# Weight statistics as traces on TensorE, later loads of wq and wk, and a new order of the early jobs

## The chip, the cores and the metric

The kernel runs on one core of a Trainium2 chip. The metric is the device time of one execution in microseconds, as the median of several runs. The kernel before takes 695.03 us (three runs, 694.98 to 695.07).

The engines are named as in the profile: PE (TensorE matmul), PEld (its weight loads), DVE (VectorE), ACT (ScalarE), POOL (GpSimd), SP (SyncE, whose queue issues nearly all DMAs).

## The reference

The sum of the input, an attention with a compressive memory, and an MLP, all on one layer norm of the input. 2048 tokens of 512 features, 32 heads of 16, four segments of 512 tokens, a hidden layer of 1792.

```python
x = A_x
xn = _layernorm(x, axis=-1)
return x + _A_ref(xn, A_wq, A_wk, A_wv, A_wo, A_beta) + _B_ref(xn, B_w1, B_b1, B_w2, B_b2)

# _A_ref, per segment s and head:
logits = einsum(qs, ks) * scale + mask            # keys at or before the query
a_dot = softmax(logits) @ vs
a_mem = (phi(qs) @ M) / (phi(qs) . z + 1e-6)      # memory of the earlier segments
o = g * a_mem + (1 - g) * a_dot;  M += phi(ks)^T vs;  z += sum(phi(ks))
...
return concat(o) @ wo
# _B_ref: y = layernorm(xn); return gelu(y @ w1 + b1) @ w2 + b2
```

## The kernel before

Everything in float32 is split into two float16 numbers, a high part and the rest, and each product is made of three matmuls (high by high, high by low, low by high). For that each weight matrix, in parts, goes through three steps before it can be used:

- `wl` (`w_load`, line 247): SP loads the raw float32 weights. They lie in the same memory that will hold the split weights, two pieces further on, or in a stage borrowed from another tile.
- `wm` (`w_square`, line 287): a sum of squares of the part, one number for each of 128 partitions. ACT squares the values (line 311) with an accumulator, which a second instruction reads.
- `wf` (`w_scale` and `qk_scale`): one or more matmuls with a matrix of ones add the partitions, ACT takes the root by logarithm and exponential (lines 320 and 321), and a few small DVE operations round it to a power of two and derive the scales.
- `ws` (`w_split`, line 358): the split of one piece of 128 x 512. In mode V, ACT writes the scaled high part (line 366) and DVE subtracts it from the scaled raw piece (line 367). In mode G, POOL scales (line 369), ACT copies to float16 (line 370), POOL subtracts (line 371).

The parts are `qk` (the first of four column pieces of wk and wq, for the first unit), `QK` (the other three), `v`, `1a` and `1b` (the halves of w1), `2a` and `2b` (the halves of w2) and `o`. `LOADS`, `SQUARES` and `SPLIT` (lines 43 to 46) say how many steps each has, and in what mode its pieces are split.

The work on data is cut into 16 units for the attention (segment by group of eight heads) and 16 for the MLP (256 tokens by half of the hidden layer). The jobs are: `X` and `Xt` layer norm and transposes, `T` the projection of a unit's queries or keys (12 matmuls of 512 columns, with copies on ACT and DVE and DMAs by SP that write strips to memory and read them back), `N` transposed keys, `V` values, `M` the maximum over logits (matmuls and a DVE reduction, line 628), `R` rows of maxima, `S` logits and their exponential, `pv` weights by values, `O` normalization, `D` seven hidden-layer matmul groups of a unit (12 matmuls of 256 columns and a DVE operation, line 756), `G` and `H` the activation and its split, `e` the second MLP layer, `out` the output projection, `A` the loading of the residual. `warm` is a job of eight matmuls on a matrix of ones (line 828) whose result is not used; there are 14 of them.

The order of all jobs is written out by hand, not found at run time: `streams()` makes one list for each kind, `ORDER` is a string with one letter for each job, and the letter says from which list the next job comes (a is the first list, c is `wts`, the loads; i is `maxi`, t is `warm`; the lists of the weight parts come last). Every engine and the SP queue execute their own instructions in this order, each waiting for what it needs. `BANKS` gives the PSUM bank of each accumulator in the same way.

In `ORDER` of the kernel before, 12 of the 14 warm-up jobs stand before the first projection T(0,1), all squares of qk and QK are spread among them, and the loads go: x, qk, QK, v, small ones, 1a, 2a, 1b.

Of the kernel before, what the change touches and what calls it, by code (L numbers as in the profile page):

```python
# [19 lines left out]
P = 128  # L20
# [8 lines left out]
NG = H // GH  # L29
# [9 lines left out]

PARTS = ("qk", "QK", "v", "1a", "2a", "1b", "2b", "o")
LOADS = {"qk": 1, "QK": 3, "v": 2, "1a": 2, "2a": 2, "1b": 3, "2b": 2, "o": 2}
SQUARES = {"qk": 2, "QK": 6, "v": 2, "1a": 3, "2a": 2, "1b": 4, "2b": 4, "o": 3}
SPLIT = {"qk": "VV", "QK": "GVGVGV", "v": "VVVV", "1a": "GVGVGVG", "2a": "GVGVGVG", "1b": "GVGVGVG", "2b": "GVGVGVG",
         "o": "GVGV"}
OFF = [0, 512, 1024, 896]
LEN = [512, 384, 256, 128]
SWAP = [(i + 16) % 32 for i in range(32)]
# [7 lines left out]
def streams():  # L57
    keys, queries, nat, maxi, soft, vals_p, heads, memo, vals, norm, again, hid, act, mlp, outs, accs, wts = (
        [] for _ in range(17))
    for i in range(NU):  # L60
        s, g = divmod(i, NG)
        keys.append(("T", i, 1))
        queries.append(("T", i, 0))
        maxi += [("M", i, n) for n in range(12)] + [("R", i)]
        for h, ts in enumerate(((0, 2), (1, 3))):
            soft += [("S", i, t, n) for t in ts for n in range(3)]
            vals_p += [("pv", i, h, kb) for kb in range(3)] + [("PV", i, h)]
        heads += [("O", i, k) for k in range(3)]
# [12 lines left out]
    again = [("ratio", n) for n in range(NSEG)]  # L81
    for j in range(NU):
        hf, fh = divmod(j, 2)
        hid += [("D", j, f) for f in range(FH)]
        act += [("G", j)] + [("H", j, c) for c in range(4)]
        if fh == 0:
            accs += [("A", 2 * hf + a, k) for a in range(2) for k in range(2)]
        mlp += [("e", j, n) for n in range(2 * FH)]
    for m in PARTS:
        wts += [("wl", m, k) for k in range(LOADS[m])]  # L90
        if m == "qk":
            wts.append(("hold",))
# [9 lines left out]
ORDER = (
    "aatcucuccvavtctveecttcetcuvaactvuvtaatcattavdtubcwwvccfwxxcxwxyxyxxgyhxcoxxvwxofooowcvwzyzoiyyiazgyyziiynzoiiys"
    "ppAnziiniicvzvcniiooAzmAihiiopzqqiqcivpqjpqjijqqijizqjiqqjiiAwszBzoAskkkkmjiAojoijsoAijAqjqjasAfoAopgkkkkpjpjqq"
    "jlpoolojjjooilihAAkkkkpaiqqiqijqjqqijqjiqjqjisBfgpiiqkkkkmpliqqiooiqpBlqoBopohijjiojiijpolsjiqaqajqiqiqqiiqapka"
    "kmkktspaqijqiqjqiqajqbqajopijjgBfopkkkBkjjjlooooBlhjjjolqiqqiipkkkkjiqqijqqjjiqiqjjqiqiqiBkkkkmpliilfnplimpngrr"
    "mrjjponijqjqjinjipiskmkkmkaiijrijjoojiqsjqqjiqiiiqqkkkkihlqlfmlogojqjqjqqjjasoojmkkkkmqjiqjqjjaojjpipmooisikkkk"
    "lpilhiofmgoooqiqpppqiqiqqqiiiqqpsosmoiqqiiqiqppsslooijqjojijojijoiaakkkkmpaijqjqjaqqqjiqqjiqjqiikmkkakbqiaqqahl"
    "olfqjjojqmjgjjoolmmkkkkmhjjoojjiitjiojiippkkkkliiilnfnimpligniinipmrrijjrsijqjqiqjiqjqiipkmkkksiqjqijqjqjiqjqii"
    "qjqikmpkkkiprlqsphlfojmjgopjjlojpjoomokmkkkqiqisjojiqisjqiqijqqijqhiqqiiqjsqiiqppmkkkkilalofomqpgopaoooospmlajq"  # L110
    "qqjqqjqjqiiqiqqqjqiqqipipooooiijooppoiaakkkkmajiqpisqqjiqjqjaiqaqhjqqqjqaaqmkkkkbjlfoljqjmjgojjqolmkkkkmmjjjooj"
    "jioijoiiippkpkkkiinliifniiilnnimlgrpmjjrmjjjrrijikkpskkiqqijqiqijqqjiqjiqjqiqjiqiispqkpkskksqilqoplfojmjgjjjpoo"
    "oojolmkkkkiqjiqpsjiqiqijqjqiqijqjiqiqiqiiqqkksmkpikplolfjjqmjgjjjoooooklpkmkkjiiopjqiqijqjiqpjqiqijqiqqiqiiqikk"
    "pspkkqiplpoooopljjjqqqjqjjqooolkpskmkpkmqqqpqjpjqqqjqjqpqqjqjqqqkmkkkqlllqqqqqqqqqrrrr"
)

BANKS = (
    "012345670123457063571265407321640573216405732164053271640527163054271630542713605427105472105427105472105472015"  # L120
    "470251407251405712470512470512470536124075631254076340125637123756123576132576132576132576132576135402761350427"
    "163054273106542736574326574326537425632754632574631072456310724563071245360712453620731620731067203617621073621"
    "073621073621037621037621037261702361475023671540263701524603175246031746013746013713460713471630471630463714067"
    "314056723410523674105236741052367410527410527410527410527410527140352671450326475103264751023674523674523647253"
    "647236547236475264735264107532410765324107265431067512043675120436751204736152047361520473615270346150312750317"
    "250317253107250371257013275027135027134650132754062751340621375460376054370567403056374065374065307645307645307"
    "642153076241076241076241076253410762534621075346210754316024310264310432610432610324610324612403246013752640163"
    "754207156437120564371205647312056473120564731206547321065473265104723607423460273460273642073642073642051736420"
    "157642031765420316750316705315631705630157630157630157306173504621357462017345620147536210436024136024316403216"
    "403216403216403216740536740536740536740536271406"  # L130
)


# [14 lines left out]
def infini_mixer_kernel(ctx: ExitStack, tc: tile.TileContext, x, wq, wk, wv, wo, beta, w1, b1, w2, b2, out):  # L148
    nc = tc.nc
    V, A, G, T, Q = nc.vector, nc.scalar, nc.gpsimd, nc.tensor, nc.sync  # L150
# [13 lines left out]
    def dense():  # L164
        return dps.tile([P, 512], F32, name="ps" + next(bank), bufs=1)
# [73 lines left out]
    def columns(w, c, n=1):
# [3 lines left out]
        return t.rearrange("p (k c) -> p k c", k=KT)  # L243

    def w_load(m, k):
        if m in ("qk", "QK"):
            g = 0 if m == "qk" else 1 + k
            for w in "kq":
                if g == 2:
                    t = sb.tile([P, 1280], F32, name="pt", bufs=4)  # L250
                    stage[w] = t[:, :512], t[:, 512:1024]
                Q.dma_start(four(piece(w, g)), columns(SRC[w], g))  # L252
            return
# [31 lines left out]
        V.memset(piece("k", 1)[:, :1], 0.0)  # L285

    def w_square(m, k):
        if m in ("qk", "QK"):
            w, g = part(m, k)
            r, junk, to = piece(w, g), WT[w][:, 1], am[:, NG * "kq".index(w) + g:NG * "kq".index(w) + g + 1]  # L290
        else:
# [19 lines left out]
        A.activation(junk.bitcast(BF)[:, :r.shape[1]], r, AF.Square, accum_out=to)  # L311

    def floor2(dst, src):

# [44 lines left out]
    def w_split(m, n):  # L359
        w, c = part(m, n)  # L360
        s = qkcol(1, "kq".index(w), c) if w in "kq" else \
            col({"v": SV, "o": SO, "1": S1, "2": S2}[w] + (m[1:] == "b"))
        r = piece(w, c)
        h, l = WT[w][:, c, 0, :], WT[w][:, c, 1, :]
        if SPLIT[m][n] == "V":
            A.activation(h, r, AF.Copy, scale=s)
            V.scalar_tensor_tensor(l, r, s, h, op0=OP.mult, op1=OP.subtract)
        else:
            G.tensor_scalar(r, r, s, 0.0, op0=OP.mult, op1=OP.add)
            A.activation(h, r, AF.Copy)  # L370
            G.tensor_tensor(l, r, h, op=OP.subtract)  # L371
# [539 lines left out]
```

## Time and profile before

| what | value |
|---|---|
| median of three runs | 695.03 us (694.98 to 695.07) |
| span of the profiled execution | 693.1 us |
| instructions in it | 16949 |
| PE busy | 678.7 us, 98% |
| DVE busy | 535.4 us, 77% |
| ACT busy | 522.7 us, 75% |
| POOL busy | 347.2 us, 50% |
| DMA | 55.12 MB, mean 80 GB/s |

The profile is of one execution. Its span, from the first to the last instruction that the profiler saw, is 693.1 us; no other time of that execution is given. The runs' median lies 1.9 us above it. A busy PE is not PE at its peak: matmuls are pipelined, their recorded durations overlap, and a group's cost is best read from the start of one group to the start of the next. In rows of a timeline the columns are start, length, engine, line, operation, what is written and read, shapes and count; in brackets stands the idle time of the engine before it and who ended it.

### The profile page before, as it was taken

What the parts mean: (1) busy time and instruction counts of PE and PEld (TensorE: products, weight loads), DVE (VectorE), ACT (ScalarE), POOL (GpSimd) and SP (SyncE); (2) the same over time, 40 slices, a digit from 0 to 9 for tenths busy, and PEclk for the clock granted to TensorE, in tenths of its full rate; (3) what the DMA queues carried; (4) which work ended last, traced back from release to release, by engine and by line L of the source; (5) the groups of instructions that cost most, each with busy time, mean ns of one, the idle gap of its engine ahead of it and who ended that gap; (6) DMA issues with size and microseconds to landing.
All of it is one profiled execution on the core that took longest, in us unless ns stands there. A gap on an engine that the chain in (4) does not pass through costs nothing.

```text
span 693.1 us, 16949 instructions
## 1 busy us (share of the span) xinstructions
PE 678.7 (98%) x6359; PEld 395.7 (57%) x6359; DVE 535.4 (77%) x1695; ACT 522.7 (75%) x1013; POOL 347.2 (50%) x533
## 2 busy tenths in 40 slices
PE   7799999999999999999999999999999999999997
PEld 6465556576654555566554456567564456656653
DVE  4499978897795887998798786888678595969442
ACT  5989898878795659857795697757795687778870
POOL 5276768365624425664334445454362546455752
PEclk9899999999999999999999999999999999999999
DMA  9984222420204213431113224231120416140101
GB/s 272 283 238 136 64 63 63 108 62 14 84 10 115 87 44 74 100 71 33 51 45 92 63 72 99 63 93 33 31 80 24 132 18 152 18 108 3 18 1 61
DMA packets 51790, 55.12 MB, mean 80 GB/s; under 512 B 4782, under 2 KB 40636, under 8 KB 51708
## 3 DMA queue, kind: packets, MB, share of 16 engines
q1 hardware_dynamic: 49404, 49.84, 25.3%
q0 software_dynamic: 2304, 4.20, 3.7%
q8 instruction: 50, 0.82, 0.5%
q14 instruction: 32, 0.26, 0.1%
HBM read 36.99 MB, written 17.04 MB: 78 GB/s over the span
## 4 chain that ended last, share of the span: by engine, by line
PE 78%; ACT 10%; POOL 4%; DVE 3%; issue 2%; DMA 1%; SPq 1%; POOLq 0%; ACTq 0%; DVEq 0%
PE ps L480 33%; PE ps L797 16%; PE ps L690 10%; PE ps L815 6%; PE ps L661 5%; PE ps L621 5%; ACT pt L666 2%; DVE ps L628 2%; PE ps L571 2%; PE ps L499 1%; ACT hT L763 1%; ACT hT L771 1%; SPq L252 1%; POOL w1s L371 1%; DMA pt<-in_A_wk_dram 1%
## 5 line engine op out<-in xcount | busy, mean ns | idle before, releaser
L628 DVE CUSTOM_DVE_ANT_0 ps<-ps,mask 128x512 f32<-128x512 f32 (+3 forms) x512 | 233.8, 522 | 16.1 <-PE ps L621 14.9
L666 ACT ACTIVATE pt<-ps,qkcs 128x512 f32<-128x512 f32 (+1 forms) x384 | 206.1, 624 | 35.3 <-PE ps L661 33.5
L797 PE MATMUL ps<-w2s,hT 64*128 64x512 f16 x1344 | 176.7, 376 | 0.2
L480 PE MATMUL ps<-xnT,w1s 128*128 128x256 f16 x1344 | 157.8, 273 | 0.0
L675 POOL TENSOR_SCALAR_AFFINE_SELECT pt<-pt 128x256 f32<-128x256 f32 x256 | 99.1, 414 | 92.0 <-ACT pt L666 91.0
L480 PEld LDWEIGHTS <-w1s 128*128 128x128 f16 x1344 | 127.3, 98 | 29.1 <-issue 11.3
L772 POOL TENSOR_TENSOR hT<-hh,hT 128x512 f16<-128x512 f32 x64 | 67.8, 1059 | 82.8 <-ACT hT L771 81.0
L797 PEld LDWEIGHTS <-hT 64*128 64x128 f16 x1344 | 76.3, 94 | 50.7 <-issue 6.0
L690 PE MATMUL ps<-pt,vt 128*32 128x512 f32 (+3 forms) x1024 | 77.3, 435 | 0.1
L756 DVE SCALAR_TENSOR_TENSOR hT<-ps,sc,sr 128x256 f32<-128x256 f32 x112 | 52.1, 478 | 27.2 <-PE ps L480 27.0
L628 DVE DVE_READ_ACCUMULATOR2_ANT mc<- 128x1 f32 x512 | 70.6, 138 | 0.0
L661 PE MATMUL ps<-qst,kst 50*128 50x512 f16 (+3 forms) x512 | 67.5, 298 | 0.3 <-ACT pt L666 0.2
L621 PE MATMUL ps<-kst,qst 48*128 48x256 f16 (+3 forms) x512 | 67.1, 297 | 0.5
L771 ACT ACTIVATE hT<-hh 128x512 f16<-128x512 f32 x64 | 36.6, 572 | 33.4 <-POOL hh L770 32.9
L690 PEld LDWEIGHTS ps<-pt,vt 128*32 128x32 f32 x1024 | 31.3, 109 | 42.4 <-issue 30.8
L770 POOL TENSOR_SCALAR hh<-hT,sc 128x512 f32<-128x512 f32 x64 | 41.8, 653 | 26.6 <-ACT hT L763 24.9
L720 POOL TENSOR_TENSOR nN<-nN,oT 128x512 f32<-128x512 f32 x16 | 20.3, 1267 | 61.3 <-DVE oT L546 61.3
L763 ACT ACTIVATE hT<-hT,b1t 128x256 f32<-128x256 f32 x112 | 46.4, 495 | 0.2
L480 PE MATMUL ps<-xnT,wqs 128*128 128x512 f16 x192 | 45.6, 389 | 0.0
L480 PE MATMUL ps<-xnT,wks 128*128 128x512 f16 x192 | 44.3, 379 | 0.0
L480 PE MATMUL ps<-wvs,xnT 128*128 128x512 f16 x192 | 44.0, 380 | 0.1
L815 PE MATMUL ps<-wos,oT 128*128 128x512 f16 x192 | 43.2, 380 | 0.6 <-POOL oT L726 0.6
(217 smaller groups left out, 890.0 us busy)
## 6 DMA issues: line engine op xcount, KB each, us to landing
kd<-hl SPq DMA_DIRECT2D x48, 128.0 KB
qd<-hl SPq DMA_DIRECT2D x48, 128.0 KB
kst<-kd SPq DMA_DIRECT2D x32, 192.0 KB
qst<-qd SPq DMA_DIRECT2D x32, 192.0 KB
acc<-in_A_x_dram SPq DMA_DIRECT2D x16, 256.0 KB
acc<-in_B_b_dram POOLq DMA_DIRECT2D x16, 256.0 KB, 4.1
out_dram<-acc SPq DMA_DIRECT2D x16, 256.0 KB
xt<-in_A_x_dram SPq DMA_DIRECT2D x14, 256.0 KB
```

Of the source, the lines that this page charges most:

```text
L480: T.matmul(p, wsl(ws, k, a), xsl(xs, k, b), start=s0 and i == 0, stop=s1 and i == 3 * n - 1)
L621: T.matmul(p[:, o:o + n], stk[i, 0][r, t, P * qb:P * qb + P], stk[i, 1][r, t, :n], start=True, stop=True)
L628: V.tensor_tensor_reduce(p[:, o:o + n], p[:, o:o + n], mask[:, 512 - n:], 1.0, -3e38, OP.add, OP.max, mc[:, 16 * b + 4 * t + qb:16 * b + 4 ...
L661: T.matmul(p[:, o:o + n], stk[i, 1][r, t, P * kb:P * kb + P], stk[i, 0][r, t, P * kb:], start=True, stop=True)
L666: A.activation(e[:, OFF[kbs[0]]:OFF[kbs[0]] + o], p[:, :o], AF.Exp, scale=qkcs[:, 1, i % NG:i % NG + 1])
L675: G.affine_select(v, v, pattern=[[0, 2], [1, P]], compare_op=OP.is_ge, fill=0.0, base=0, channel_multiplier=-1)
L690: T.matmul(p[32 * c:32 * c + 32, P * kb:], vt[s, kb][:, 4 * g + c, 16 * odd:16 * odd + 32], pt[i, 2 * c + odd][:, OFF[kb]:OFF[kb] + LEN[kb ...
L756: V.scalar_tensor_tensor(hz[:, fi, :], p[:, :256], col(F1 + fh), srow[hs][:, own], op0=OP.mult, op1=OP.mult)
L763: A.activation(z, z, AF.Gelu_apprx_tanh, bias=b1t[:, FH * (j % 2) + f:FH * (j % 2) + f + 1])
L772: G.tensor_tensor(hT[:, z, 1, :], t, hT[:, z, 0, :], op=OP.subtract)
L797: w = T.matmul(pes[j][a], hTs[fh][r, fi, u, P * a:P * a + P], w2s[r, fo, v, :], start=n == 0 and m == 0, stop=fi == FH - 1 and m == 2, ski ...
L815: T.matmul(p, o[:, u, P * b:P * b + P], wos[:, g, v, :], start=i == 0, stop=i == 3 * NG - 1)
```

## The change

The sums of squares of qk, QK, v, 1a and 2a (all but that of the bias b1) are no longer made on ACT. Each block of 128 columns of the raw weights, read as the upper halves of its float32 values (bfloat16), is multiplied with its own transpose on PE, and the products are added up in one PSUM bank; the sum of squares is the trace of that matrix, which DVE takes with a multiplication by the identity and a sum along the row.

QK is now the second column piece alone; the third and the fourth are a new part, RK, with loads of its own that stand later in the order, a scale of its own and a list of its own. The job that computes the gates moves from the list of v to that of RK.

A new mode P of the split has POOL write the scaled high part as float16 at once, and DVE subtract. It takes the place of G, and of some V, in QK, RK, v, 1a and 2a: counting the two V of qk, which stay, 15 pieces are P and 11 are V, where 11 were G and 15 V.

The first 270 jobs come in a new order; from T(3,1) on the order is that of before. Four of the twelve warm-up jobs that precede T(3,1) now stand after T(0,1): two right behind it, one behind D(0,6), one behind T(2,1). The loads go: x, qk, QK, v, small ones, 1a, 2a, then RK in two steps (behind T(0,1) and behind T(0,0)), 1b. The seven jobs D(0,0) to D(0,6) come before the first M. The letters of the weight lists shift by one, since u is now the list of RK's loads.

```diff
@@ -39,11 +39,12 @@
 
 
 
-PARTS = ("qk", "QK", "v", "1a", "2a", "1b", "2b", "o")
-LOADS = {"qk": 1, "QK": 3, "v": 2, "1a": 2, "2a": 2, "1b": 3, "2b": 2, "o": 2}
-SQUARES = {"qk": 2, "QK": 6, "v": 2, "1a": 3, "2a": 2, "1b": 4, "2b": 4, "o": 3}
-SPLIT = {"qk": "VV", "QK": "GVGVGV", "v": "VVVV", "1a": "GVGVGVG", "2a": "GVGVGVG", "1b": "GVGVGVG", "2b": "GVGVGVG",
+PARTS = ("qk", "QK", "v", "1a", "2a", "RK", "1b", "2b", "o")
+LOADS = {"qk": 1, "QK": 1, "RK": 2, "v": 2, "1a": 2, "2a": 2, "1b": 3, "2b": 2, "o": 2}
+SQUARES = {"qk": 2, "QK": 2, "RK": 4, "v": 2, "1a": 3, "2a": 2, "1b": 4, "2b": 4, "o": 3}
+SPLIT = {"qk": "VV", "QK": "PV", "RK": "PPPP", "v": "VPVP", "1a": "PVPVPVP", "2a": "PVPVPVP", "1b": "GVGVGVG", "2b": "GVGVGVG",
          "o": "GVGV"}
+TRACES = ("qk", "QK", "RK", "v", "1a", "2a")
 OFF = [0, 512, 1024, 896]
 LEN = [512, 384, 256, 128]
 SWAP = [(i + 16) % 32 for i in range(32)]
@@ -87,47 +88,48 @@
             accs += [("A", 2 * hf + a, k) for a in range(2) for k in range(2)]
         mlp += [("e", j, n) for n in range(2 * FH)]
     for m in PARTS:
-        wts += [("wl", m, k) for k in range(LOADS[m])]
+        if m != "RK":
+            wts += [("wl", m, k) for k in range(LOADS[m])]
         if m == "qk":
             wts.append(("hold",))
         if m == "v":
             wts.append(("par",))
     split = [[("wm", m, k) for k in range(SQUARES[m])] + [("wf", m)] + [("ws", m, c) for c in range(len(SPLIT[m]))] +
-             [("gate",)] * (m == "v") for m in PARTS]
+             [("gate",)] * (m == "RK") for m in PARTS]
     zero = [("zero", 0), ("const",), ("zero", 1)]
     return [norm, again, wts, [("par2",)], zero, keys, queries, nat, maxi, soft, vals_p, heads, memo, vals, hid, act,
-            mlp, outs, accs, [("warm", n) for n in range(14)]] + split
+            mlp, outs, accs, [("warm", n) for n in range(14)], [("wl", "RK", k) for k in range(2)]] + split
 
 
 ORDER = (
-    "aatcucuccvavtctveecttcetcuvaactvuvtaatcattavdtubcwwvccfwxxcxwxyxyxxgyhxcoxxvwxofooowcvwzyzoiyyiazgyyziiynzoiiys"
...
+    "atacctcaetcttetcawvavcatwvcaxeacatxvdccwvxwfttyyyxbxyyuxgyyyzozoywouoxyccyzhoAzzAootAAppciiizAznpBiiABfBncAiBpi"
+    "gzBszniipnzBiimchqqqiCBqBqiiioAoACBCCBCjjqiojqAjqjcioijoiCikskkBcmDskioBjiqiqCjjoijqCiqjsCqjDiftaoCCpgkkkpkjqCj"
+    "oloojjljoloojiipkkkkiqihspqijqqipqijqiqjsjqqjaajfgpiiqkkkkmpliqqiooiqpDlqoDopohijjiojiijpolsjiqaqajqiqiqqiiqapk"
+    "akmkktspaqijqiqjqiqajqbqajopijjgDfopkkkDkjjjlooooDlhjjjolqiqqiipkkkkjiqqijqqjjiqiqjjqiqiqiDkkkkmpliilfnplimpngr"
+    "rmrjjponijqjqjinjipiskmkkmkaiijrijjoojiqsjqqjiqiiiqqkkkkihlqlfmlogojqjqjqqjjasoojmkkkkmqjiqjqjjaojjpipmooisikkk"
...
 )
 
 
 
 BANKS = (
-    "012345670123457063571265407321640573216405732164053271640527163054271630542713605427105472105427105472105472015"
...
+    "050123614061756123401632157467410534702651305176254301741260523716405142730612547306651240651024615024612504612"
...
 )
 
 
@@ -228,12 +230,12 @@
         n = PIECES[m]
         return flat(m)[:, 512 * c + 1024:512 * c + 1536] if c < n - 2 else stage[m][c - n + 2]
 
+    QKG = {"qk": 0, "QK": 1, "RK": 2}
+
     def part(m, c):
 
-        if m == "qk":
-            return "kq"[c], 0
-        if m == "QK":
-            return "kq"[c % 2], 1 + c // 2
+        if m in QKG:
+            return "kq"[c % 2], QKG[m] + c // 2
         return m[0], c + (FH if m[1:] == "b" else 0)
 
     def columns(w, c, n=1):
@@ -243,8 +245,8 @@
         return t.rearrange("p (k c) -> p k c", k=KT)
 
     def w_load(m, k):
-        if m in ("qk", "QK"):
-            g = 0 if m == "qk" else 1 + k
+        if m in QKG:
+            g = QKG[m] + k
             for w in "kq":
                 if g == 2:
                     t = sb.tile([P, 1280], F32, name="pt", bufs=4)
@@ -285,7 +287,7 @@
         V.memset(piece("k", 1)[:, :1], 0.0)
 
     def w_square(m, k):
-        if m in ("qk", "QK"):
+        if m in QKG:
             w, g = part(m, k)
             r, junk, to = piece(w, g), WT[w][:, 1], am[:, NG * "kq".index(w) + g:NG * "kq".index(w) + g + 1]
         else:
@@ -308,7 +310,17 @@
             junk = junk.rearrange("p n a c -> p (n a c)")
         else:
             junk = junk.rearrange("p a c -> p (a c)")
-        A.activation(junk.bitcast(BF)[:, :r.shape[1]], r, AF.Square, accum_out=to)
+        if m not in TRACES or r is b1t:
+            A.activation(junk.bitcast(BF)[:, :r.shape[1]], r, AF.Square, accum_out=to)
+            return
+        p = dense()
+        v = r.bitcast(BF).rearrange("p (c a) -> p c a", a=2)[:, :, 1]
+        n = r.shape[1]
+        for c in range(0, n, P):
+            u = v[:, c:min(c + P, n)]
+            T.matmul(p[:u.shape[1], :u.shape[1]], u, u, start=c == 0, stop=c + P >= n)
+        c = min(P, n)
+        V.tensor_tensor_reduce(p[:c, :c], p[:c, :c], ident[:c, :c], 1.0, 0.0, OP.mult, OP.add, to[:c])
 
     def floor2(dst, src):
 
@@ -333,8 +345,8 @@
         V.scalar_tensor_tensor(qkcs[:, 1, g0:g0 + n], f[:, 0], float(2 ** 10), f[:, 1], op0=OP.mult, op1=OP.mult)
 
     def w_scale(m):
-        if m in ("qk", "QK"):
-            return qk_scale(*((0, 1) if m == "qk" else (1, NG - 1)))
+        if m in QKG:
+            return qk_scale(QKG[m], 1 + (m == "RK"))
         h = m[1:] == "b"
         nb = m[0] == "1"
         n = 4 if h else 3 if m == "o" else 2
@@ -362,7 +374,10 @@
             col({"v": SV, "o": SO, "1": S1, "2": S2}[w] + (m[1:] == "b"))
         r = piece(w, c)
         h, l = WT[w][:, c, 0, :], WT[w][:, c, 1, :]
-        if SPLIT[m][n] == "V":
+        if SPLIT[m][n] == "P":
+            G.tensor_scalar(h, r, s, 0.0, op0=OP.mult, op1=OP.add)
+            V.scalar_tensor_tensor(l, r, s, h, op0=OP.mult, op1=OP.subtract)
+        elif SPLIT[m][n] == "V":
             A.activation(h, r, AF.Copy, scale=s)
             V.scalar_tensor_tensor(l, r, s, h, op0=OP.mult, op1=OP.subtract)
         else:
```

More of the change, by code (lines that the diff above doesn't have):

```diff
@@ L102 @@
 ORDER = (
-    "aatcucuccvavtctveecttcetcuvaactvuvtaatcattavdtubcwwvccfwxxcxwxyxyxxgyhxcoxxvwxofooowcvwzyzoiyyiazgyyziiynzoiiys"
[L104 to L112, printed above, removed]
@@ L113 @@
-    "oojolmkkkkiqjiqpsjiqiqijqjqiqijqjiqiqiqiiqqkksmkpikplolfjjqmjgjjjoooooklpkmkkjiiopjqiqijqjiqpjqiqijqiqqiqiiqikk"
-    "pspkkqiplpoooopljjjqqqjqjjqooolkpskmkpkmqqqpqjpjqqqjqjqpqqjqjqqqkmkkkqlllqqqqqqqqqrrrr"
+    "atacctcaetcttetcawvavcatwvcaxeacatxvdccwvxwfttyyyxbxyyuxgyyyzozoywouoxyccyzhoAzzAootAAppciiizAznpBiiABfBncAiBpi"
+    "gzBszniipnzBiimchqqqiCBqBqiiioAoACBCCBCjjqiojqAjqjcioijoiCikskkBcmDskioBjiqiqCjjoijqCiqjsCqjDiftaoCCpgkkkpkjqCj"
+    "oloojjljoloojiipkkkkiqihspqijqqipqijqiqjsjqqjaajfgpiiqkkkkmpliqqiooiqpDlqoDopohijjiojiijpolsjiqaqajqiqiqqiiqapk"
@@ new lines @@
+    "akmkktspaqijqiqjqiqajqbqajopijjgDfopkkkDkjjjlooooDlhjjjolqiqqiipkkkkjiqqijqqjjiqiqjjqiqiqiDkkkkmpliilfnplimpngr"
+    "rmrjjponijqjqjinjipiskmkkmkaiijrijjoojiqsjqqjiqiiiqqkkkkihlqlfmlogojqjqjqqjjasoojmkkkkmqjiqjqjjaojjpipmooisikkk"
+    "klpilhiofmgoooqiqpppqiqiqqqiiiqqpsosmoiqqiiqiqppsslooijqjojijojijoiaakkkkmpaijqjqjaqqqjiqqjiqjqiikmkkakbqiaqqah"
+    "lolfqjjojqmjgjjoolmmkkkkmhjjoojjiitjiojiippkkkkliiilnfnimpligniinipmrrijjrsijqjqiqjiqjqiipkmkkksiqjqijqjqjiqjqi"
+    "iqjqikmpkkkiprlqsphlfojmjgopjjlojpjoomokmkkkqiqisjojiqisjqiqijqqijqhiqqiiqjsqiiqppmkkkkilalofomqpgopaoooospmlaj"
@@ L115 @@
+    "qqqjqqjqjqiiqiqqqjqiqqipipooooiijooppoiaakkkkmajiqpisqqjiqjqjaiqaqhjqqqjqaaqmkkkkbjlfoljqjmjgojjqolmkkkkmmjjjoo"
+    "jjioijoiiippkpkkkiinliifniiilnnimlgrpmjjrmjjjrrijikkpskkiqqijqiqijqqjiqjiqjqiqjiqiispqkpkskksqilqoplfojmjgjjjpo"
+    "ooojolmkkkkiqjiqpsjiqiqijqjqiqijqjiqiqiqiiqqkksmkpikplolfjjqmjgjjjoooooklpkmkkjiiopjqiqijqjiqpjqiqijqiqqiqiiqik"
+    "kpspkkqiplpoooopljjjqqqjqjjqooolkpskmkpkmqqqpqjpjqqqjqjqpqqjqjqqqkmkkkqlllqqqqqqqqqrrrr"
 )
 BANKS = (
-    "012345670123457063571265407321640573216405732164053271640527163054271630542713605427105472105427105472105472015"
@@ L121 @@
[L121 to L130, printed above, removed]
+    "050123614061756123401632157467410534702651305176254301741260523716405142730612547306651240651024615024612504612"
@@ new lines @@
+    "504650124650412650412650412650142650142650421607653420107642531076425031702531270531270531270132570132570132576"
+    "135402761350427163054273106542736574326574326537425632754632574631072456310724563071245360712453620731620731067"
+    "203617621073621073621073621037621037621037261702361475023671540263701524603175246031746013746013713460713471630"
+    "471630463714067314056723410523674105236741052367410527410527410527410527410527140352671450326475103264751023674"
+    "523674523647253647236547236475264735264107532410765324107265431067512043675120436751204736152047361520473615270"
@@ new lines @@
+    "346150312750317250317253107250371257013275027135027134650132754062751340621375460376054370567403056374065374065"
+    "307645307645307642153076241076241076241076253410762534621075346210754316024310264310432610432610324610324612403"
+    "246013752640163754207156437120564371205647312056473120564731206547321065473265104723607423460273460273642073642"
+    "073642051736420157642031765420316750316705315631705630157630157630157306173504621357462017345620147536210436024"
+    "136024316403216403216403216403216740536740536740536740536271406"
```

## The prediction

> **What bounds the kernel now.** I read the page first, then the busy time by stretch, then the timeline of each engine in the first 124 us.
>
> ```profile
> span 693.1 us, 16949 instructions
> ...
> PE 678.7 (98%) x6359; PEld 395.7 (57%) x6359; DVE 535.4 (77%) x1695; ACT 522.7 (75%) x1013; POOL 347.2 (50%) x533
> ...
> PE   7799999999999999999999999999999999999997
> ...
> ACT  5989898878795659857795697757795687778870
> ...
> PEclk9899999999999999999999999999999999999999
> ```
>
> PE is the bound from the third slice on. The first two slices are different: much of what PE does there is warm-up (line 828), and one slice shows a lower clock. The stretches below are cut at three marks: A, 19.18 us, where the first key projection starts on PE; B, 33.96, the first hidden-layer job D(0,0); C, 123.52, the key projection T(3,1). From T(3,1) on the job order of the two kernels is the same, 1038 jobs, so what the change is worth is by how much C moves.
>
> ```profile
> 0.00:19.18 19.18, 15.18 (x121) 12.67 (x122) 8.88 (x30) 11.95 (x31) 8.93 (x23) 1.00 0.96 274
> 19.18:33.96 14.78, 9.88 (x49) 5.55 (x46) 6.00 (x28) 14.47 (x27) 4.35 (x5) 0.77 0.96 295
> 33.96:80.00 46.04, 45.54 (x382) 26.40 (x380) 44.64 (x151) 41.75 (x83) 31.50 (x37) 1.00 0.55 159
> 80.00:123.52 43.52, 43.52 (x457) 26.86 (x457) 34.05 (x106) 39.38 (x80) 30.59 (x48) 1.00 0.23 57
> 123.52:693.10 569.58, 564.62 (x5361) 324.26 (x5358) 441.86 (x1383) 415.13 (x797) 271.80 (x422) 1.00 0.24 63
> ```
>
> Columns: length, then busy time of PE, PEld, DVE, ACT, POOL, granted clock, DMA share, GB/s. From A to B ACT is busy 14.47 of 14.78 us: it squares and splits weights, and PE waits for it. From B to 80 us PE (45.54 of 46.04) and DVE (44.64) are both full; from 80 to C PE alone.
>
> ```profile
> 17.86 1.05 PE L828 MATMUL ps<-ones 128*128 128x256 f16 x8
> 18.75 0.60 PE L433 MATMUL ps<-ident,rat 128*128 128x128 f32 x4
> 19.18 2.91 PE L480 MATMUL ps<-xnT,wks 128*128 128x512 f16 x12
> 21.93 0.71 PE L343 MATMUL ps<-am,ones 128*128 128x1 f32 x4
> 25.95 0.59 PE L343 MATMUL ps<-am,ones 128*128 128x1 f32 x2 [3.31 <-ACT w1s L311]
> 27.77 0.59 PE L343 MATMUL ps<-am,ones 128*128 128x1 f32 x2 [1.23 <-ACT w1s L311]
> ...
> 28.64 4.18 PE L480 MATMUL ps<-xnT,wqs 128*128 128x512 f16 x12
> ...
> 33.25 0.38 PE L343 MATMUL ps<-am,ones 128*128 128x1 f32 x2 [0.31 <-ACT w2s L311]
> 33.56 0.47 PE L499 MATMUL ps<-ident,phk 64*128 64x64 f32 x8
> 33.96 2.79 PE L480 MATMUL ps<-xnT,w1s 128*128 128x256 f16 x24
> 36.59 2.75 PE L480 MATMUL ps<-xnT,wks 128*128 128x512 f16 x12
> 39.18 5.40 PE L480 MATMUL ps<-xnT,w1s 128*128 128x256 f16 x48
> ```
>
> ```profile
> 50.78 1.14 PE L343 MATMUL ps<-am,ones 128*128 128x1 f32 x8
> 51.78 0.36 PE L345 MATMUL ps<-am,ones 128*128 128x1 f32 x2
> ...
> 123.52 2.76 PE L480 MATMUL ps<-xnT,wks 128*128 128x512 f16 x12
> ```
>
> PE's real work from A to B: two projections at 2.75 (row 36.59; the one at 28.64 took 4.18 at a clock of 0.77), 14 matmuls of scales (21.93 to 33.25) at 0.125 (eight from 50.78 to 51.78), and 0.40 of transposes (33.56 to 33.96): 5.5 + 1.75 + 0.4 = 7.65. So 14.78 - 7.65 = 7.1 us are lost to ACT. That, and what lies ahead of A, is all that the change can win before B.
>
> **The change part by part.**
>
> *ACT.* 14 squares with their accumulator reads leave ACT (8 of 512 columns, two of 1024, four of 1792), and 15 of its 26 copies for splits. At the rows of two of them (1.70 us for 1792 columns, 0.63 for 512, below) that is about 5 + 2 + 7 for squares and 9 for copies. ACT no longer limits anything up to B. Worth nothing by itself where PE is full, so it counts as the 7.1 us above.
>
> ```profile
> 9.81 0.63 ACT L311 ACTIVATE wks<-wks 128x512 bf16<-128x512 f32 x1 [0.27 <-DMA wks<-in_A_wk_dram]
> ...
> 10.44 0.19 ACT L397 ACTIVATE nw<-nw 128x8 f32<-128x8 f32 x1
> ...
> 16.41 2.01 ACT L469 ACTIVATE xnT<-ps 128x512 f16<-128x512 f32 x4
> ...
> 24.10 1.70 ACT L311 ACTIVATE w1s<-w1s 128x1792 bf16<-128x1792 f32 x1
> ```
>
> ```profile
> 8.07 0.53 DVE L396 TENSOR_SCALAR nw<-ag 128x4 f32<-128x4 f32 x1
> ...
> 33.84 0.75 DVE L367 SCALAR_TENSOR_TENSOR w1s<-w1s,sc 128x512 f16<-128x512 f32 x1 [3.68 <-ACT w1s L366]
> ...
> 37.92 0.81 DVE L367 SCALAR_TENSOR_TENSOR w1s<-w1s,sc 128x512 f16<-128x512 f32 x1 [0.39 <-ACT w1s L366]
> 38.65 1.17 DVE L367 SCALAR_TENSOR_TENSOR wqs<-wqs,qksc 128x512 f16<-128x512 f32 x1
> ...
> 49.17 0.32 DVE L628 CUSTOM_DVE_ANT_0 ps<-ps,mask 128x128 f32<-128x128 f32 x1
> 49.42 0.13 DVE L628 DVE_READ_ACCUMULATOR2_ANT mc<- 128x1 f32 x1
> ```
>
> *Mark A.* The norm's logarithm waited on ACT from 8.60 (8.07 + 0.53) to 10.44 behind squares, and the four copies into xnT from the transposes' end to 16.41. Now neither waits. What stands in front is PE's own queue: the first trace needs the second key piece, whose landing ACT saw at 9.81; from there, in order, 12 + 4 + 16 traces (below: 0.08 each, 2.6), four groups of transposes at 0.43 (row 18.75 to 19.18: 1.7), two warm-up jobs at 0.89 (17.86 to 18.75: 1.8) and the first scale 0.25: 9.81 + 6.35 = 16.2. Then DVE has the last trace's reduction (0.25) and the key split (0.75): 17.2 with no gap. Upper end: 19.18, as before. I take 18.0, since DVE has the first scale's chain and four xnT halves to pass in the same time: -1.2.
>
> *Traces on PE.* A piece of n columns takes n/128 matmuls of 128x128, each with its own weights. After A stand 28 of w1, 28 of w2, 16 of the later wq and wk: 72. No such matmul is in the trace. Bounds: half of a 256-column one with its own weights (row 39.18: 5.40/48 = 0.1125, half 0.056), and the f32 transposes of 128 columns (0.43/4 = 0.108). The middle, 0.08, is what I take, since the columns say the first and a weight load per matmul the second: 72 x 0.08 = +5.8 (4.0 to 7.8).
>
> *Warm-up jobs.* Before, all 12 that precede C stand before A, where PE has nothing else. Now eight do; two follow T(0,1), one follows D(0,6), one T(2,1). 4 x 0.89 = +3.6 if PE has work to do there, nothing if it would wait.
>
> *Small ones on PE.* The row-scale transposes move behind A (+0.43), the scale of wv ahead of it (four at 0.125, -0.5), RK has a scale of its own (two, +0.25): +0.2.
>
> *DVE.* 11 more subtractions (0.75: 8.3), 14 reductions of traces at 0.25 (49.17 to 49.42: 3.5), six small operations for RK at no more than that (1.5): +13.3 on 93.6 (8.88 + 6.00 + 44.64 + 34.05), that is 106.9 by C. From A, with some 10 done before it, 97 of the 106.8 us that the sum below leaves: 91%. It fits, but the stretch B to 80 stays as full as it was; so I let the waits that it hides stay as they are.
>
> *POOL.* 22 operations of the old G splits (0.69 and 1.2) become 15 P's.
>
> ```profile
> 32.73 0.69 POOL L369 TENSOR_SCALAR w1s<-w1s,sc 128x512 f32<-128x512 f32 x1
> 34.41 1.20 POOL L371 TENSOR_TENSOR w1s<-w1s 128x512 f16<-128x512 f32 x1 [0.98 <-ACT w1s L370]
> ...
> 38.15 1.13 POOL L369 TENSOR_SCALAR w1s<-w1s,sc 128x512 f32<-128x512 f32 x1
> ```
>
> POOL gets freer by 22 x 0.95 - 15 x 0.69 = 10 us. But each P runs beside DVE's subtractions. The trace has that pairing: POOL's 38.15 took 1.13 instead of 0.69, DVE's 38.65 1.17 instead of 0.75, while DVE's 37.92, also beside it, took 0.81. DVE is free enough up to B (6.00 of 14.78 busy), so the eight P's of 2a and RK count: between 8 x 0.06 = 0.5 and 8 x 0.42 = 3.4. I take 0.5, the price of the pair in which DVE was first; the 9% of DVE's time that are free can take up the rest.
>
> [...]
>
> *Queues.* SP: the loads of RK (four of 256 KB) leave their place before wv. At about 295 GB/s (row A to B) 1.05 MB come 3.6 us earlier for wv, w1, w2. Nobody waited for them (the square at 24.10 shows no idle time before it), so that hides. RK's loads now stand behind the strip DMAs of T(0,1) and T(0,0), which wait for ACT and DVE; behind them are the loads of 1b, and RK's traces wait for them after D(0,4). The strips of T(0,0) leave SP some 7 us after it in the old trace, and PE has D(0,0) to D(0,4) for as long: hidden, and if not, a delay of 1 to 2 us. POOL's queue gets nothing new to issue.
>
> **The sum.** C after = 18.0 + 7.65 + 89.56 (B to C as it was) + 5.8 + 3.6 + 0.2 = 124.8, against 123.52: +1.3. With 0.5 for POOL beside DVE: +1.8. The span of the profiled execution is 693.1; the runs' median is 695.03, 1.9 above it, so I add the difference to the median: 696.8. In words: the 7.1 us that PE lost to ACT, and 1.2 at the start, are filled with 9.6 us of new matmuls that stand in PE's own queue.
>
> **The rivals.**
>
> 1. *The fillers are free* (faster). If PE would wait at those four places for DVE or for a landing, the warm-up jobs cost nothing. For: the two after T(0,1) stand before traces whose sum DVE must first reduce behind T(0,1)'s own evictions. Against: w1 has landed by then, and PE is never idle from B to C. 696.8 - 3.6 = 693.2; it decides when 3.2 of the 3.6 are free.
> 2. *Traces at the low end* (no change). At 0.056 they cost 4.0: 696.8 - 1.8 = 695.0. For: weight loads lie beside matmuls everywhere (PEld 57% beside PE 98%). Against: here each matmul is as short as its load.
> 3. *DVE becomes the bound* (slower still). With the full 0.42 on eight P's 1.3 + 3.4 gives 699.7. For: DVE is at 97% from B to 80 already. Against: ACT, which it waited for, is free. [...]
>
> **How the numbers follow.** What a measurement of this kernel can tell from no change is about 0.2%, 1.4 us. Forecast 0.42, of which 0.30 lies above +1.4 us and 0.12 below it; rival 1 0.22; rival 2 0.22; rival 3 0.14. Faster 0.22, same 0.12 + 0.22 = 0.34, slower 0.30 + 0.14 = 0.44. The likeliest case by itself: 695.6 to 698. The range goes down to rival 1 with part of rival 2's saving, 692.7, and up to rival 3 with the traces in the middle, 699.8.
>
> **What would show it.** A at 17 to 19; about 72 new 128x128 matmuls after it at 0.06 to 0.11, without ACT as releaser of the scale matmuls; D(0,0) at about 30 instead of 33.96 (18.0 + 2.75 + 1.8 + 28 traces 2.2 + 0.43 + 0.75 + 2.75 + 14 traces 1.1 = 29.8), yet T(3,1) at 124 to 126. Line 367 on DVE longer than 0.75 in the mean, and P's longer than 0.69. I am wrong if PE shows idle time of 2 us or more between A and 50 us in which the warm-ups hide, if T(3,1) comes before 122, or if the stretch after T(3,1) does not take 569.6.

## The result, and the profile after

The changed kernel takes 691.43 us (median of four runs, 691.08 to 691.68), the kernel before, beside it, 695.0 (694.78 to 695.07). The ratio is 0.9945, 95% interval 0.9931 to 0.996: faster by about 3.6 us. The forecast was 696.8, on the other side of no change, and the time lies below the range that was given. Two more sets of runs of the same kernel, on other chips, gave 692.28 (ratio 0.9965, 0.9953 to 0.9978) and 692.11 (0.9959, 0.9947 to 0.9971); they are the measure for the experiments that ran beside them.

The page of the changed kernel, the lines that answer to those shown of before:

```profile
span 689.8 us, 17163 instructions
...
PE 681.8 (99%) x6465; PEld 399.8 (58%) x6465; DVE 545.7 (79%) x1740; ACT 502.9 (73%) x972; POOL 340.5 (49%) x526
...
PE   8999999999999999999999999999999999999997
...
ACT  4486897788786659856794796766795687878870
...
PEclk9999999999999999999999999999999999999999
```

PE's second slice is now full, ACT's first two went from 5 and 9 to 4 and 4, and no slice has a lower clock. The stretches between the marks A (T(0,1) starts on PE), B (D(0,0)), 80 us and C (T(3,1)); columns as before: length, then PE, PEld, DVE, ACT, POOL, granted clock, DMA share, GB/s.

```profile
0.00:15.95 15.95, 13.80 (x122) 11.70 (x123) 9.77 (x42) 6.83 (x13) 8.95 (x23) 1.00 0.95 275
15.95:26.36 10.41, 10.41 (x95) 7.39 (x95) 9.47 (x35) 5.43 (x15) 3.06 (x4) 1.00 1.01 326
26.36:80.00 53.64, 52.89 (x505) 33.77 (x506) 51.46 (x177) 38.41 (x79) 27.88 (x37) 1.00 0.55 161
80.00:120.20 40.20, 40.20 (x408) 23.54 (x395) 31.94 (x102) 35.83 (x70) 26.96 (x41) 1.00 0.31 74
120.20:689.80 569.60, 564.53 (x5360) 323.40 (x5358) 443.10 (x1387) 416.39 (x799) 273.68 (x424) 1.00 0.24 63
```

A moved from 19.18 to 15.95, B from 33.96 to 26.36, C from 123.52 to 120.20, and the stretch after C takes 569.60 against 569.58. So C's 3.32 us are the whole change in the span (693.1 to 689.8). All of it was there at A already (3.23): from A to C the kernel before took 104.34, the one after 104.25. Within that, A to B is 4.4 shorter (14.78 to 10.41) and B to C 4.3 longer (89.56 to 93.84). In the profiles of the two other sets C is at 120.70 and 120.18. PE in that first part:

```profile
9.44 0.62 PE L321 MATMUL ps<-wks 128*128 128x128 bf16 x8 [0.55 <-DMA wks<-in_A_wk_dram]
...
10.57 1.04 PE L843 MATMUL ps<-ones 128*128 128x256 f16 x8
...
13.68 1.04 PE L843 MATMUL ps<-ones 128*128 128x256 f16 x8
...
15.10 0.23 PE L855 MATMUL ps<-ident,mhl 14*128 14x14 f32 x1
15.26 0.38 PE L338 MATMUL ps<-am,ones 128*128 128x2 f32 x2
15.50 0.58 PE L355 MATMUL ps<-am,ones 128*128 128x1 f32 x4
15.95 2.75 PE L495 MATMUL ps<-xnT,wks 128*128 128x512 f16 x12
18.53 1.91 PE L843 MATMUL ps<-ones 128*128 128x256 f16 x16
20.28 1.77 PE L321 MATMUL ps<-w1s 128*128 128x128 bf16 x28
21.89 0.60 PE L448 MATMUL ps<-ident,rat 128*128 128x128 f32 x4
22.32 0.56 PE L355 MATMUL ps<-am,ones 128*128 128x1 f32 x4
...
22.96 2.75 PE L495 MATMUL ps<-xnT,wqs 128*128 128x512 f16 x12
25.55 0.97 PE L321 MATMUL ps<-w2s 128*128 128x128 bf16 x14
26.36 1.47 PE L495 MATMUL ps<-xnT,w1s 128*128 128x256 f16 x12
```

No row from A on has a wait of ACT in its brackets. The 28 traces of w1 stand from 20.28 to 21.89, 1.61 us, 57.5 ns each; the two warm-up jobs of 18.53 take 1.75.

### The profile page after: what moved, and what is told of

It reads as the page before. It is cut to its first block, busy times and chain, and to the rows that moved or that the text cites. A ratio compares the mean times of both kernels' runs of the same rounds, so it can differ in the third digit from the quotient of the medians.

```text
span 689.8 us, 17163 instructions
## 1 busy us (share of the span) xinstructions
PE 681.8 (99%) x6465; PEld 399.8 (58%) x6465; DVE 545.7 (79%) x1740; ACT 502.9 (73%) x972; POOL 340.5 (49%) x526
## 4 chain that ended last, share of the span: by engine, by line
PE 85%; DVE 5%; ACT 5%; DMA 2%; POOL 1%; issue 1%; SPq 0%; POOLq 0%; DVEq 0%; ACTq 0%
PE ps L495 36%; PE ps L812 17%; PE ps L705 10%; PE ps L830 6%; PE ps L676 5%; PE ps L636 5%; DVE ps L643 3%; ACT pt L681 2%; PE ps L586 2%; PE ps L514 1%; PE ps L843 1%; PE ps L321 1%; DMA wks<-in_A_wk_dram 1%; DMA qd<-hl 1%; PE ps L617 1%
## 5 line engine op out<-in xcount | busy, mean ns | idle before, releaser
L690 POOL TENSOR_SCALAR_AFFINE_SELECT pt<-pt 128x256 f32<-128x256 f32 x256 | 101.0, 421 | 98.2 <-ACT pt L681 97.2
L495 PEld LDWEIGHTS <-w1s 128*128 128x128 f16 x1344 | 127.2, 98 | 28.5 <-issue 11.6
L495 PE MATMUL ps<-xnT,wqs 128*128 128x512 f16 x192 | 44.2, 380 | 0.0
```

The costliest lines, as they stand in the source:

```text
L495: T.matmul(p, wsl(ws, k, a), xsl(xs, k, b), start=s0 and i == 0, stop=s1 and i == 3 * n - 1)
L690: G.affine_select(v, v, pattern=[[0, 2], [1, P]], compare_op=OP.is_ge, fill=0.0, base=0, channel_multiplier=-1)
```

## The experiments

The question is what the 3.3 us at C are made of. My theory was that statistics on TensorE take work out of ACT's queue, where PE waited for it, and that this is the gain (Q in the expectations). The rivals: the new order and the later loads do it by themselves, whatever computes the statistics (O); the warm-up jobs behind A stand where PE would wait anyway (F); DVE sets the pace (D); later, the two last warm-up jobs cost time where they stand (W). All kernels below are the changed kernel with one edit, but for the last, which is the kernel before with one edit.

**Squares back on ACT, the new order kept.**

```diff
-        if m not in TRACES or r is b1t:
+        if m in TRACES and r is not b1t:
+            next(bank)
+        if True:
             A.activation(... AF.Square, accum_out=to)
```

The squares of RK, where ACT makes them, write their unused results to a place of their own.

> The changed kernel with all the squares back on ACT (new order, later RK loads and P splits stay; no trace matmuls). Theory Q (PE's own queue sets the time from A to T(3,1), and what the traces bring is that nothing before D(0,0) waits for ACT): 4.2 us of trace matmuls leave PE, but the squares of 1a and 2a (7 us) stand on ACT between A and D(0,0), where ACT has 5 of 10.4 us free: A slips by 1 to 2 us, 3 to 6 us of waits come in, 691.5 to 695. Rival O (the new order alone makes the gain, squares or traces alike): PE is rid of 4.2 us, 687 to 688.

702.14 us, ratio 1.0092 (1.0077 to 1.0106): 10 us slower than the changed kernel, which ran on other chips (692.28 and 692.11), 7 slower than the kernel before beside it, and above what either theory gave. PE's rows (first fence) and its busy time by stretch (second):

```profile
19.42 0.61 PE L497 MATMUL ps<-xnT,wks 128*128 128x512 f16 x2 [0.23 <-ACT wks L383]
...
26.82 0.38 PE L357 MATMUL ps<-am,ones 128*128 128x1 f32 x2 [0.41 <-ACT w1s L316]
28.64 0.38 PE L357 MATMUL ps<-am,ones 128*128 128x1 f32 x2 [1.44 <-ACT w1s L316]
```

```profile
20.00:30.00 10.00, 7.96 (x41) 4.65 (x41) 5.92 (x23) 6.74 (x14) 1.88 (x2) 0.83 0.70 237
```

A is at 19.42, about where it was before the change (19.18), PE waits for the squares of w1 as it did before, and the clock falls to 0.83. The new order, loads and splits without the traces (O) do not gain: they lose.

Two kernels put only half of the squares back: those of w1 and w2, and those of wk, wq and wv.

```diff
+        act = m in TRACES and r is not b1t and m in ("1a", "2a")      # the other: not in
+        if act:
+            next(bank)
-        if m not in TRACES or r is b1t:
+        if act or m not in TRACES or r is b1t:
```

> The changed kernel with the squares of 1a and 2a alone back on ACT (4 squares of 1.8 us with their reads, 3.2 us of traces less on PE; qk, QK, RK and v stay traces). A stays at 16 to 17. Theory Q (what the traces bring is that nothing behind A waits for ACT): D(0,0) 2 to 4 us later, 3 to 5 us slower than the changed kernel. If the traces of w1 and w2 only cost PE time: 2 to 3 us faster.

> The changed kernel with the squares of qk, QK, RK and v alone back on ACT (1a and 2a stay traces). Up to A it is the kernel with all squares on ACT, whose A was 19.42: so A 2.6 to 3.5 us later, and with RK's squares and its scale on ACT another 1 to 3: 3.5 to 6 us slower than the changed kernel. With the run before, the two parts should add to about the 10 us of all squares, if they do not overlap.

698.54 us (1.0054, 1.0041 to 1.0067) and 699.94 (1.0075, 1.0062 to 1.0088); the changed kernel beside them 692.11. So 6.4 and 7.8, both above what was expected; the two together are 14.2 where all squares cost 10, so they overlap. The profiled execution with the squares of w1 and w2 is the fastest of its five (696.49); from A (16.19) to C (124.56) it takes 108.37, 4.1 more than the changed kernel. The rows of PE with the squares of w1 and w2 on ACT show what I had left out of the price:

```profile
21.88 0.38 PE L358 MATMUL ps<-am,ones 128*128 128x1 f32 x2 [0.76 <-ACT w1s L317]
23.70 0.38 PE L358 MATMUL ps<-am,ones 128*128 128x1 f32 x2 [1.44 <-ACT w1s L317]
...
24.29 4.44 PE L498 MATMUL ps<-xnT,wqs 128*128 128x512 f16 x12
```

PE waits 2.2 us, and then the projection T(0,0) takes 4.44 us where row 22.96 of the changed kernel has 2.75 for the same: these waits are paid a second time in the clock, as the stretch shows. Together that is 3.9 of the 4.1 us.

```profile
20.00:30.00 10.00, 7.80 (x41) 4.36 (x38) 5.89 (x15) 7.26 (x14) 2.45 (x3) 0.83 0.62 212
```

With the squares of wk, wq and wv on ACT it is A that comes late (19.01), as with all squares.

**Warm-up jobs left out.** First the four behind A, then the last two, at 154 and 350 us.

```diff
     def warm_up(n):
+        if 8 <= n <= 11:        # the other kernel: 12 <= n <= 13
+            next(bank)
+            return
```

> The changed kernel without the four warm-up jobs behind T(0,1), D(0,6) and T(2,1). Theory Q: PE has work there, so all of their 3.5 us comes off, 687.9. Rival F (fillers: PE would wait there for DVE or a landing in any case): 691.0 to 691.5. Between: 689.5 if the two behind T(0,1) alone hide.

693.39 us (0.9973, 0.9962 to 0.9983): nothing gained. From A (16.80) to C (121.19) it takes 104.39, the changed kernel 104.25, with 3.5 us less of work on PE. Where they went:

```profile
16.80 2.75 PE L495 MATMUL ps<-xnT,wks 128*128 128x512 f16 x12
19.39 0.48 PE L321 MATMUL ps<-w1s 128*128 128x128 bf16 x3
...
21.20 1.61 PE L321 MATMUL ps<-w1s 128*128 128x128 bf16 x25 [1.33 <-DMA w1s<-in_B_w_dram]
```

PE gets to the traces of w1 at once, does three, and waits 1.33 us for the rest of w1 to land. F holds: the two fillers behind T(0,1) stand for the most part in that wait, and what the other two free is gone in waits by C. A is 0.85 later than in the first profile for another reason, told under the hardware below.

> The changed kernel without its last two warm-up jobs (154 and 350 us), which stand where PE shows no idle time around them; the four of the first experiment stay. Theory W (a filler is free only where PE waits for a landing or another engine at that very place, as for w1 at 20 us): here both come off, 2 x 0.88 = 1.8 us faster than the changed kernel beside it. Rival (PE's time is elastic everywhere, other engines take up what is saved): within 0.5 us of it.

692.26 us (0.9957, 0.9945 to 0.9969) beside 692.11: no gain here either. The changed kernel first, then this one, both as PE's rows:

```profile
154.49 1.05 PE L843 MATMUL ps<-ones 128*128 128x256 f16 x8
155.47 0.82 PE L812 MATMUL ps<-w2s,hT 64*128 64x512 f16 x6
...
157.21 0.43 PE L636 MATMUL ps<-kst,qst 48*128 48x384 f16 x4
```

```profile
154.64 0.82 PE L812 MATMUL ps<-w2s,hT 64*128 64x512 f16 x6
...
157.33 0.41 PE L636 MATMUL ps<-kst,qst 48*128 48x384 f16 x3 [0.79 <-ACT nD L714]
```

The work after the filler comes 0.83 earlier and then waits 0.79 for ACT. W falls. PE shows 99% busy in both; a row that says busy doesn't say needed.

**The 72 traces behind A done twice** (the second pass starts the sum anew, so the result is the same).

```diff
-        for c in range(0, n, P):
+        for c in [*range(0, n, P)] * (2 if m in ("1a", "2a", "RK") else 1):
```

> The changed kernel with each trace of 1a, 2a and RK computed twice on PE (72 matmuls more, all behind A; the result is the same). Theory Q: 72 x 0.058 = +4.2 us, 695.6. Rival D (DVE sets the pace from A to 80 us and hides PE's extra): under +1.5 us.

700.49 us (1.0067, 1.0052 to 1.0081). From A (16.31) to C (127.97) it takes 111.66, 7.4 more, for 72 x 0.0575 = 4.1 us of work: nearly twice what was expected. From A to T(1,1) the extra is just the extra traces (10.41 + 16.86 = 27.27 became 12.82 + 18.59 = 31.41, +4.1). Then, where no trace was added, T(1,1) to T(2,1): the changed kernel first.

```profile
43.22:88.84 45.62, 44.87 (x433) 25.57 (x431) 43.78 (x160) 35.19 (x73) 26.36 (x37) 1.00 0.38 118
```

```profile
47.72:96.94 49.22, 46.61 (x432) 26.22 (x431) 45.05 (x160) 34.76 (x72) 26.44 (x36) 0.97 0.37 109
```

3.6 us more: 1.9 are PE's waits (49.22 - 46.61 against 45.62 - 44.87) and 1.7 are the same matmuls taking longer at a clock of 0.97. D falls: if DVE set the pace, more work on PE would have been free. Why the waits grow there, where DVE (mc, 1.0) and a read-back of strips (qst, 0.7 twice) are late, was not settled.

**The loads of RK back ahead of wv, w1 and w2.**

```diff
 ORDER: the two letters u (loads of RK) stand behind the third c (load of QK) again
```

> The changed kernel with the four loads of RK back in their old place, ahead of wv, w1 and w2 (nothing else moved). The prediction's step (1.05 MB earlier for wv, w1, w2, but nobody waits for them, so it hides): 691 to 692. Theory L (the run without warm-ups shows PE waiting until 21.2 us for w1; so the landings of wv and w1 set the front of the kernel, and the old squares hid that because ACT came later still): wv's and w1's traces start about 3.6 us later, 694.5 to 696.

695.69 us (1.0004, 0.9995 to 1.0013), the changed kernel beside it 692.28: 3.4 slower, as much as the whole change gains.

```profile
15.30 0.63 PE L310 MATMUL ps<-wvs 128*128 128x128 bf16 x8 [2.67 <-DMA wvs<-in_A_wv_dram]
...
20.51 2.75 PE L484 MATMUL ps<-xnT,wks 128*128 128x512 f16 x12
```

The traces of wv stand in PE's queue ahead of the last transposes of the norm. With 1.05 MB in front of it wv lands 2.67 us too late, everything behind it waits, and A is at 20.51 instead of 16.82. From A to C it takes 103.96, so the loss is all ahead of A: wv's traces start 2.1 us later (15.30, beside 13.21), and 1.6 more go on the matmuls behind them at a lower clock (0.83 from 10 to 20 us).

**Splits.** The pieces in mode P (POOL writes the high part, DVE subtracts) in mode G, as most were before, or in V.

```diff
-  "QK": "PV", "RK": "PPPP", "v": "VPVP", "1a": "PVPVPVP", "2a": "PVPVPVP"
+  each P as G        # the other kernel: all pieces V
```

> The changed kernel with mode G in place of P in all 15 pieces (POOL scales, ACT copies, POOL subtracts; DVE has 15 subtractions less). If DVE is what limits A to 80 us: 688 to 691. Theory C (what counts is the way from a weight's trace to its split pieces, which G makes longer, 2.5 us instead of 1.5 a piece and 1.9 instead of 0.7 us of POOL): the hidden-layer jobs D(0,0) to D(0,6) wait for pieces, 694 to 698.

> The changed kernel with mode V in place of P in all 15 pieces (ACT writes the high part instead of POOL; ACT has some 10 us more to do, POOL 10 less, and nothing of POOL runs beside DVE's subtractions). If POOL beside DVE costs what the forecast put in (0.5) or more: 688 to 691. If the pieces' way through ACT, which also has the evictions, is the longer one: 692 to 694.

With G 710.04 us (1.0214, 1.02 to 1.0228), 18 slower, far above what was expected. What PE waited for, from 28 to 110 us: us in total, times, longest.

```profile
PE ps L355 <- ACT w2s L314: 4.0, 3, 2.9
PE ps L636 <- ACT fa L332: 2.9, 1, 2.9
```

ACT is late again: the longest wait (2.9 us) is for its squares of w2's second half, and ahead of these in ACT's queue stand two of the copies that G needs, which wait for POOL:

```profile
79.32 0.63 ACT L385 ACTIVATE wks<-pt 128x512 f16<-128x512 f32 x1 [1.86 <-POOL pt L384]
81.89 0.63 ACT L385 ACTIVATE wqs<-pt 128x512 f16<-128x512 f32 x1 [1.94 <-POOL pt L384]
82.43 1.04 ACT L314 ACTIVATE w2s<-w2s 128x1024 bf16<-128x1024 f32 x1
```

From D(0,0) to T(2,1) the kernel takes 17.75 us more than the changed one (80.23, 62.48); 10.7 of them are waits of PE, and 7.0 the same matmuls at a lower clock (0.96 from 28.40 to 52.80 us, 0.82 from there to 66, 0.76 from 80 to 94). With V 694.52 (0.9993, 0.9983 to 1.0003), 2.2 slower, the loss spread over D(0,0) to T(3,1) (95.70 us, the changed kernel beside it 93.47). P is the cheapest of the three.

**The kernel before with traces, its order, splits and loads kept** (the statistics of qk, QK, v and of the first halves of w1 and w2 as traces, each in the PSUM bank least recently used).

```diff
-        A.activation(... AF.Square, accum_out=to)
+        traces of the part and their reduction on DVE, as in the changed kernel
```

> The kernel before, in its old order and with its old splits and loads, with traces on PE in place of the squares of qk, QK, v, 1a and 2a. Theory Q: A comes 2 to 3 us earlier, the 7.1 us of waits behind A shrink to what the G splits of 1a leave (1.66 us a piece on POOL), and 4 us of traces are added, part of them in waits: 691 to 693. Rival O (order, P splits and loads are what pays): 694.5 to 696.

706.94 us (1.0167, 1.0154 to 1.018): 11.6 slower than before. Q was expected at 691 to 693 and missed badly. Its 1.66 us of POOL for a G piece is low, too: in the trace of the kernel before the piece of rows 32.73 and 34.41 took 0.69 + 1.20.

```profile
7.08 0.61 PE L328 MATMUL ps<-wks 128*128 128x128 bf16 x4 [3.60 <-DMA wks<-in_A_wk_dram]
...
11.29 0.58 PE L328 MATMUL ps<-wks 128*128 128x128 bf16 x4 [2.82 <-DMA wks<-in_A_wk_dram]
...
31.61 2.75 PE L499 MATMUL ps<-xnT,wks 128*128 128x512 f16 x12 [1.46 <-DVE am L330]
```

In the old order the traces stand ahead of the norm's transposes, and PE's queue waits for each piece to land (6.8 us); A comes at 31.61. Ahead of A PE also waits 2.9 us for DVE's reductions (am), part of which may come from the choice of banks, so 11.6 is the price of this version and not the least possible. As built, neither half pays alone: the new order, loads and splits without traces lose 7, the traces without them 11.6, both together gain 3.

## Why the prediction was wrong, point by point

**What was right.** The tail after C did not move (569.60). ACT no longer releases anything up to B, so the 7.1 us went. The four warm-up jobs behind A do take 3.5 us of PE's time. PE's idle time behind B stayed small: from B to 80 us 0.5 us before (46.04 - 45.54), 0.75 after (53.64 - 52.89). DVE is at 96% there (51.46 of 53.64), as full as before, and did not become the bound.

**What failed is the sum**, 125.3 at C with POOL's half microsecond, against 120.2: a wait for DVE ahead of A that did not come, and terms that were put too high, all on one side:

- *Mark A: 18.0 forecast, 15.95 measured, below the lower bound of 17.2.* The path was wrong: I let A wait for DVE, 1.0 us for the last reduction and split and 0.8 for its chain, but PE has no idle time from 9.44 to A and waited for neither (1.8 less). What ends last there is PE's own queue, and I had left 0.85 of it out of this sum (rows 15.10 to 15.95; the scale of wv stood only among the small ones). Besides, the first trace starts at 9.44, not 9.81 (0.4 less), and the 32 traces ahead of A take 1.9 us, not 2.6 (0.6 less). Together that is 1.95 of the 2.05 us. DVE's split of the key piece is the first row here; it ends at 16.23, when the projection is already running, so the first matmuls of that did not wait for it:

```profile
15.48 0.75 DVE L382 SCALAR_TENSOR_TENSOR wks<-wks,qksc 128x512 f16<-128x512 f32 x1
...
17.77 1.12 DVE L382 SCALAR_TENSOR_TENSOR wqs<-wqs,qksc 128x512 f16<-128x512 f32 x1
19.07 0.75 DVE L379 SCALAR_TENSOR_TENSOR wks<-wks,qksc 128x512 f16<-128x512 f32 x1
```

- *Traces: 0.08 taken, 0.0575 measured*, near the low end 0.056 (half of a 256-column matmul). The 72 behind A take 4.2 by the starts of their rows, instead of 5.8. Rival 2 had this and stood at 0.22. A weight load for every matmul does not show in the time: the loads of the 28 of w1 lie beside their matmuls, which run from 20.28 to 21.89, 57.5 ns each.

```profile
20.17 1.70 PEld L321 LDWEIGHTS <-w1s 128*128 128x128 bf16 x28
```

- *POOL beside DVE: 0.5 taken (up to 3.4), no cost to PE found.* The pairs do get longer. DVE's rows are the last two above, these are POOL's:

```profile
17.66 0.69 POOL L378 TENSOR_SCALAR wks<-wks,qksc 128x512 f16<-128x512 f32 x1 [5.20 <-issue]
...
19.25 1.14 POOL L378 TENSOR_SCALAR wvs<-wvs,sc 128x512 f16<-128x512 f32 x1 [0.90 <-DVE sc L361]
```

  DVE's instruction at 17.77 began while POOL's of 17.66 was running and took 1.12 instead of 0.75; POOL's at 19.25 ran into DVE's split of 19.07 and took 1.14 instead of 0.69. So the pairs are as the sum had them, but rival 3 (699.7), which follows from them, did not come: all of PE's idle time from A to C is 0.75 us, so that longer DVE rows can have made PE wait no more than that. With V in place of P, where ACT and not POOL writes the high parts, the kernel is 2.2 us slower; that run moves work to ACT too, so it does not price the pairs by themselves.

- *The rest, about 1,* is spread over A to C: the two projections before B, for one, take 2.6 us each to the start of the next row (18.53 - 15.95; 25.55 - 22.96), where the sum had 2.75, a row's length. A row's length holds the end that overlaps the next row; starts are what adds up. The remainder was not followed row by row.

**Two steps were wrong in kind, not in size.** *"That hides"*, of the 1.05 MB that no longer stand ahead of wv, w1 and w2, was argued from the old trace, where nobody waited for them. The new order has PE wait for exactly these: 3.4 us with the loads back in front. The later loads are not a side effect of the change but a condition of it; the sum was not moved by this, since with the loads moved nobody waited. And rival 1's counter-argument, *"w1 has landed by then"*, was false: with the fillers gone PE waits for w1 until 21.20. So rival 1's mechanism is right. That the fillers' 3.6 us still belonged in the sum is because the sum had no waits in their place: left out, they give way to waits of 3.3 us (1.33 for w1, the others at most 0.7 each), where the changed kernel has 0.75. Of my signs of being wrong, T(3,1) before 122 came true; idle time of PE in which the fillers hide appears only when they are left out.

**Where the gain is.** By A: 3.23 us, since ACT's squares no longer delay the norm (A at 19.42 with them) and wv lands in time for its traces (A at 20.51 without). That fewer warm-up jobs stand ahead of A does not do it alone: eight and the squares on ACT give 19.42, twelve gave 19.18. From A to C the 7.1 us of ACT are used up by 4.2 of traces and by 3.5 of fillers that stand where PE would wait for landings and DVE. Two warm-up jobs still stand ahead of A (rows 10.57 and 13.68, 1.75 us to the starts of what follows) in a stretch without idle time of PE; whether A would come earlier without them was not tested.

## What to carry to other kernels

Moving work to another engine's queue moves what that queue waits for: here traces on PE are 10 us better than squares on ACT in one order and 11.6 worse in another, so order, loads and engine must be costed as one change, landing by landing. "Nobody waited for this transfer" holds for the old order only. And before charging filler work in a busy engine, ask when what follows it is there: only leaving the filler out shows whether it costs anything.

## What the runs showed of the hardware

*A wait of PE can be paid twice.* In several runs the clock dropped where PE had little to do for some microseconds, and the next matmuls took longer: 0.83 over ten microseconds with all squares on ACT and with those of w1 and w2 (from 20 to 30 us), and with RK's loads in front (from 10 to 20 us); 4.44 us for a projection of 2.75. The kernel before had it too: PE waited 3.31 us ahead of its row 25.95, the clock was 0.50 from 24.75 to 31.50 us, row 28.64 took 4.18, and that is part of the 7.1 us. If the clock was 0.50 in the other kernels as well, 0.83 over ten microseconds is 10 x 0.17 / 0.5 = 3.4 us of it, and 1.7 us lost each time, an estimate from these figures; by its row the projection lost as much (4.44 - 2.75). The kernel with the traces done twice has 0.83 too, from 70 to 80 us, and lost the same 1.7. PE was not wholly idle ahead of it: in the kernel with the squares of w1 and w2 it did six small matmuls from 21.88 on, behind waits of 0.76 and 1.44 us. The changed kernel shows no drop in its profile (1.00 in every stretch), and a wait of 1.33 us by itself, in the kernel without the four fillers (mean clock 1.0), did not do it either. How much waiting it takes was not shown.

*The start moves by itself.* In three profiles of the same changed kernel A was at 15.95, 16.82 and 16.14. In the first and the third the first traces wait for a piece of wk to land; in the second the profile names DVE's norm, which had itself waited 1.11 us for rows of x. Of the 0.87 us by which A came later in the second, 0.50 were left at C (120.70 beside 120.20); an edit worth less than a microsecond is better read from A to C than from the whole time.
